# Second MLP's weight blocks: raw words loaded a step ahead, low halves kept in the norm's slots

## The chip, the cores and the metric

The kernel runs on one core of one Trainium2 chip. The metric is the time of one execution on the device in microseconds (us), the median of several runs. A core has five engines that each work through a list of their own, in order: PE (matmuls; its weight loads are shown as PEld), DVE (VectorE), ACT (ScalarE), POOL (GpSimd) and SP, which here only issues DMAs. An engine that waits for a semaphore holds up everything behind it in its list.

## The reference

Attention with two kinds of masks feeds a block with a Fourier mix and an MLP, whose result feeds a token-mixing block with a second MLP:

```
x = attention(q, k, v)                       # 4 batches, 576 tokens, 512 channels
u = x + real(fft(fft(x, tokens), channels))
x = u + relu(norm(u) @ moe_w_ch1) @ moe_w_ch2             # 512 -> 2048 -> 512
u = x + (relu(x^T @ moe2_w_tok1) @ moe2_w_tok2)^T         # 576 -> 256 -> 576
out = u + relu(u @ moe2_w_ch1) @ moe2_w_ch2               # 512 -> 1536 -> 512
```

The weights arrive as float64. The kernel reads them as pairs of 32-bit words.

## The kernel before, in words

The tokens of four batches make 18 tiles of 128 rows. The first MLP works in six chunks c = 0 to 5 of three tiles each, and in 16 slices f of its hidden width. One step (c, f) in `run` is `gemm1` (12 matmuls of 384 columns, L414), an activation that writes `hh`, the high half of the hidden values (ACT, L418), a subtraction that writes `hl`, the low half (DVE, L419), and `gemm2` (9 matmuls of 512 columns, L433). Every product is taken from high and low halves, since PE reads rounded fp32.

Beside the steps of the chunks 2 to 4 the kernel gets the second MLP's weights ready. They are cut into 24 blocks: 12 of w1 (L101's source `in_w1b_dram`) and 12 of w2 (`in_w2b_dram`), one begun every second step, in turns. A block goes through these stages:

- `words` loads four pieces of raw words into a tile `wraw` (SP, L101). ACT takes the absolute value of the high words (L106), four DVE instructions make a float of the pair (L108, L111, L112, L113). The result is `wu`.
- `sums` makes four sums or differences for Strassen's scheme on POOL (L147; w2 has one more, L149) into a tile `wt4`. ACT rounds both to high halves (L153), written back into `wraw`. POOL subtracts to get the low halves `wbl` (L154). Two DMAs store high and low halves to DRAM (`wsd`, L156), from where `load_ops` fetches them for the last stage (L685).

`blocks` is a generator: `begin` runs it to its first pause (loads issued), each `advance` to its next. The pool `wstage` has a ring of three raw buffers (tag "raw") and one of two (tag "wu"). In the kernel before a block takes two of the three raw buffers, one for `wraw` and one for `wbl`:

```
raw = wstage.tile([P, 512, 2], I32, tag="raw", name="wraw", bufs=3)
lo  = wstage.tile([P, 1024], F32R, tag="raw", name="wbl", bufs=3)
```

In the last chunk, c = 5, the six token weights (`load_wt`, `in_wt_dram`) go through `words` and the same rings, and `c_load` begins to split the input of the next stage into `ch` (ACT, L725) and `cl` (DVE or POOL, L726). After the steps come the token products (L785 `tk`, L807 `tu`) and the second MLP (L896, L1037).

The norm of the first MLP takes its output tile `lm` from a ring of three in the pool `lp` (ACT, L485), three times a chunk.

The order of each engine's list is not written out here. The program is recorded in source order, and a scheduler then places instructions by its own model of durations; `behind` adds an order without a wait (L106 and L153 behind the latest `hh`, L108 behind the latest `hl`). So an edit in the source moves instructions on several engines.

Of the kernel before, what the change touches and what calls it, by code (L numbers as in the profile page):

```python
# [10 lines left out]
F32R = mybir.dt.float32r  # L11
# [3 lines left out]
ALU = mybir.AluOpType  # L15
# [3 lines left out]
DM = 512  # L19
P = 128  # L20
# [3 lines left out]
NCH = 6  # L24
# [14 lines left out]
def f32(ap):  # L39
    return ap.bitcast(F32)  # L40
# [3 lines left out]
def attention_fourier_mlp_kernel(ctx: ExitStack, tc: tile.TileContext, a: dict, out: bass.AP):  # L44
    nc = tc.nc

    const = ctx.enter_context(tc.tile_pool(name="const", bufs=1, side="left"))
    wstage = ctx.enter_context(tc.tile_pool(name="wstage", bufs=2, side="left"))
# [17 lines left out]
    wsd = {w: [dram.tile([7, P, 512], F32, name=f"wsd{w}{m}") for m in range(NP2)] for w in "12"}  # L66
# [7 lines left out]
    def behind(ins, prev):  # L74

        if prev is not None:
            tc.add_manual_dep(ins.ins, prev.ins.name, mybir.DependencyInfo(
                mybir.DependencyClass.NoSync, mybir.DependencyReason.SCHED_ONLY), reason="order of the stream")
# [6 lines left out]
    def advance():  # L85
        for x in list(under_way):
            if next(x, None) is None:
                under_way.remove(x)

    def begin(x):  # L90
        next(x)
        under_way.append(x)
# [3 lines left out]
    def words(srcs, eng):  # L96
        raw = wstage.tile([P, 512, 2], I32, tag="raw", name="wraw", bufs=3)
        n = 0
        for src in srcs:
            w = src.shape[1] // 2  # L100
            behind(nc.sync.dma_start(out=raw[:, n:n + w], in_=src.rearrange("p (c t) -> p c t", t=2)), hold[0])  # L101
            n += w
        yield 1
        low, high = raw[:, :n, 0], raw[:, :n, 1]
        u = wstage.tile([P, 512], I32, tag="wu", name="wu", bufs=2)[:, :n]
        behind(nc.scalar.activation(out=f32(u), in_=f32(high), func=AF.Abs, scale=2.0**16), relu.get("hh"))  # L106
        v = nc.vector
        clamp = eng().tensor_scalar(f32(u), f32(u), E_MIN, E_MAX, op0=ALU.max, op1=ALU.min)  # L108
        if eng() is v:
            behind(clamp, relu.get("hl"))  # L110
        v.tensor_scalar(u, u, 4, 1, op0=ALU.logical_shift_left, op1=ALU.logical_shift_right)  # L111
        v.scalar_tensor_tensor(out=u, in0=high, scalar=-2**31, in1=u, op0=ALU.bitwise_and, op1=ALU.bitwise_or)  # L112
        v.scalar_tensor_tensor(out=u, in0=low, scalar=29, in1=u, op0=ALU.logical_shift_right, op1=ALU.bitwise_or)  # L113
        yield f32(u), raw
# [12 lines left out]
    def blocks(w, m, c0):  # L127
        src = a["w" + w + "b"]
        order = ((0, 256), (0, 0), (1, 0), (1, 256)) if w == "2" else ((1, 0), (0, 0), (0, 256), (1, 256))
        x = words([src[m + NP2 * i][:, 2 * (c + c0):2 * (c + c0) + 256] for i, c in order], lambda: nc.vector)  # L130
        yield next(x)
        u, raw = next(x)
        yield 1
        sums(w, m, c0, u, raw)

    def sums(w, m, c0, u, raw):
        q = [u[:, 128 * i:128 * i + 128] for i in range(4)]
        t = wstage.tile([P, 512], F32, tag="wu", name="wt4", bufs=2)
        t1, t2, t3, t4 = (t[:, 128 * i:128 * i + 128] for i in range(4))
        if w == "2":  # L140
            b12, b11, b21, b22 = q
            todo = ((t1, b12, b11, 0), (t2, b22, t1, 0), (t3, b12, b22, 0), (t4, t2, b21, 0))
        else:
            a21, a11, a12, a22 = q
            todo = ((t1, a21, a22, 1), (t2, t1, a11, 0), (t3, a11, a21, 0), (t4, a12, t2, 0))
        for o, x, y, plus in todo:
            nc.gpsimd.tensor_tensor(out=o, in0=x, in1=y, op=ALU.add if plus else ALU.subtract)  # L147
        if w == "2":
            nc.gpsimd.tensor_scalar_mul(q[3], q[3], -1.0)  # L149
        hi = raw.rearrange("p c t -> p (c t)").bitcast(F32R)  # L150
        lo = wstage.tile([P, 1024], F32R, tag="raw", name="wbl", bufs=3)
        for x, s in ((u[:, 128:512], slice(0, 384)), (t, slice(384, 896))):
            behind(nc.scalar.activation(out=hi[:, s], in_=x, func=AF.Copy), relu.get("hh"))  # L153
            nc.gpsimd.tensor_tensor(out=lo[:, s], in0=x, in1=f32(hi[:, s]), op=ALU.subtract)  # L154
        for x, o in ((hi, c0), (lo, 256 + c0)):
            nc.sync.dma_start(out=wsd[w][m][:, :, o:o + 128].rearrange("b p c -> p b c"),  # L156
                              in_=f32(x[:, :896]).rearrange("p (b c) -> p b c", c=128))


    lt = [(0, t) for t in range(6)]  # L160
# [330 lines left out]
    if True:  # L491
# [8 lines left out]
        lp = dst.enter_context(tc.tile_pool(name="ln", bufs=1, side="right"))  # L500
# [28 lines left out]
        f = fp.tile([P, 2, 3, 512], F32R, name="f")  # L529
# [24 lines left out]
        def load_wa():  # L554
            if order:
                x, f = order.pop(0)
                pool, tag = (wa, "wa") if f < 4 else (wx, "wx") if f < 8 else (wb, "wb") if f < 12 else (wc, "wc")
                begin(slot_w(a["w1a" if x == "1" else "w2a"][f], pool, tag, "wA",
                             lambda *t, w=w1 if x == "1" else w2: w.__setitem__(f, t)))
# [20 lines left out]
        for gno, g in enumerate(gl):  # L580
            b, gi = g.b, g.gi
# [54 lines left out]
        def last_fft(x):  # L636
            nonlocal wb, wc
            x4 = four[3]
            prev = relu["hh"], relu["hl"]
            if 2 <= x < 5:  # L640
                x4.prep(x - 2, prev[1], prev[0])
            x4.after = prev
            for mt in {4: (0,), 5: (1, 2), 6: (3, 4)}.get(x, ()):
                x4.s1(mt)
            for i in {7: (0, 1, 2)}.get(x, ()):
                x4.s2(i)
            if x == 8:
                fst.close()
                wb = wbst.enter_context(tc.tile_pool(name="wb", bufs=16, side="left", reuse_waits="tile"))
                wc = wcst.enter_context(tc.tile_pool(name="wc", bufs=16, side="left", reuse_waits="tile"))  # L650
# [8 lines left out]
        def load_wt():  # L659
            n0 = len(wt_names)  # L660
            if n0 < 6:
                nm, i = "12"[n0 // 3], n0 % 3
                wt_names.append(nm)
                src = a["wt" + nm]
                n = min(512, src.shape[1] // 2 - 512 * i)

                def done(hi, lo):
                    wt["h" + nm, i], wt["l" + nm, i] = hi, lo

                begin(slot_w(src[:, 1024 * i:1024 * i + 2 * n], wa, "wa", "wt", done, n))  # L670
# [57 lines left out]
        def c_load(b, ts, late=0):  # L728
            for x, t in enumerate(ts[:4] if b % 2 else ts):
                if late:  # L730
                    begin(c_tile(b, t, late + x // 2))
                else:
                    list(c_tile(b, t, 0))
# [19 lines left out]
        def extra1(c, f):  # L753
            if steps.index((c, f)) <= 8:
                last_fft(steps.index((c, f)))
            advance()
            load_wa()
            if 2 <= c < NCH - 1 and f % 4 == 1:
                m, h = divmod((c - 2) * 4 + f // 4, 2)
                begin(blocks("2", m, 128 * h))  # L760
            if 2 <= c < NCH - 1 and f % 4 == 3:
                m, h = divmod((c - 2) * 4 + f // 4, 2)
                begin(blocks("1", m, 128 * h))
            if c == NCH - 1:
                if f >= 1:
                    load_wt()
                if f == 2:
                    c_load(0, range(3), 3)
                if f == 9:
                    c_load(1, range(5), 3)  # L770

        steps = [(c, f) for h in range(len(PARTS) - 1) for c in range(2) for f in range(PARTS[h], PARTS[h + 1])]
        steps += [(c, f) for c in range(2, NCH) for f in range(NF1)]
        run(m1, steps, prep1, fin1, extra1)


# [452 lines left out]
```

## Time and profile before

| what | value |
|---|---|
| median of 3 runs | 920.49 us (919.70 to 922.67) |
| profiled execution | 919.07 us, of which the span from first to last instruction is 917.3 us |
| PE busy | 889.0 us, 97% of the span |
| DVE, ACT, POOL busy | 561.9, 407.7, 306.7 us |
| granted TensorE clock, mean | 0.994 |

The span is nearly all PE. What is to be had is in PE's few pauses, and these are read by stretch: which stretch has them, and which engine ended each. Times in the rows are counted from the start of the span. The chunks 2 to 4 run from about 300 to 510 us, chunk 5 to about 586 us.

### The profile page before, as it was taken

Reading aid. Unit: us, or ns where it says so; the run is one execution under the profiler, and the core shown is the slowest. Engines: PE = TensorE matmul, PEld = TensorE weight load, DVE = VectorE, ACT = ScalarE, POOL = GpSimd, SP = SyncE. Lnnn points to the kernel's source line nnn. Section 1 sums busy time; section 2 is a strip of 40 time slices with the busy share of each in tenths; the row PEclk is TensorE's granted clock in tenths of the full one; section 3 lists DMA queues with packets and bytes.
Section 4 is the critical chain, followed back from the end, with each engine's and each line's share of the span. In section 5 each row is a group of like instructions: output and inputs, shape, how many; then the busy total and the mean of one; then the engine's idle time right before and its main releaser. Section 6 shows DMA issues by size and latency. Waiting matters only on the chain.

```text
span 917.3 us, 15396 instructions
## 1 busy us (share of the span) xinstructions
PE 889.0 (97%) x5554; PEld 826.3 (90%) x5554; DVE 561.9 (61%) x1049; ACT 407.7 (44%) x1067; POOL 306.7 (33%) x377
## 2 busy tenths in 40 slices
PE   7989998999999999999999999899999999999997
PEld 6979998989998998898988887687999999999997
DVE  4677999797993444534433446846344444898774
ACT  6978884443432233233223224324355545444432
POOL 4431321332330134344344333510113002946660
PEclk9989999999999999999999999999999999999999
DMA  9998764334432444644744766588733287146351
GB/s 264 313 275 256 217 197 134 111 130 144 138 92 70 126 144 139 195 127 131 230 128 133 224 183 183 184 284 293 236 128 147 95 279 235 37 162 226 131 196 46
DMA packets 115987, 159.69 MB, mean 174 GB/s; under 512 B 9643, under 2 KB 69873, under 8 KB 115911
## 3 DMA queue, kind: packets, MB, share of 16 engines
q1 hardware_dynamic: 113111, 153.07, 52.6%
q0 software_dynamic: 2544, 5.42, 2.3%
q8 instruction: 44, 0.72, 0.3%
q14 instruction: 32, 0.26, 0.1%
q10 hardware_dynamic: 256, 0.21, 0.1%
HBM read 103.61 MB, written 55.06 MB: 173 GB/s over the span
## 4 chain that ended last, share of the span: by engine, by line
PE 54%; DVE 11%; DMA 7%; POOL 3%; ACT 3%; issue 3%; SPq 3%; POOLq 0%; DVEq 0%; ACTq 0%
PE oo L1037 14%; PE oo L433 9%; PE h L414 9%; PE z L896 8%; PE y L896 4%; DMA wraw<-in_w1b_dram 4%; POOL wt L147 3%; PE tu L807 3%; DVE wu L112 2%; PE tk L785 2%; PE w L896 2%; DVE wu L113 2%; SPq L101 2%; DVE wu L108 2%; ACT wraw L153 1%
## 5 line engine op out<-in xcount | busy, mean ns | idle before, releaser
L414 PE MATMUL h<-uT,wAh 128*128 128x384 f32 x768 | 203.9, 339 | 0.1
L414 PEld LDWEIGHTS h<-uT,wAh 128*128 128x128 f32 x768 | 139.9, 189 | 4.9 <-DVE uT L404 0.4
L1037 PE MATMUL oo<-wo,ht 128*128 128x256 f32 x972 | 133.7, 281 | 0.0
L414 PE MATMUL h<-uT,wAl 128*128 128x384 f32 x384 | 129.6, 338 | 0.0
L1037 PEld LDWEIGHTS oo<-wo,ht 128*128 128x128 f32 x972 | 126.5, 189 | 0.0
L433 PE MATMUL oo<-wAh,hh 128*128 128x512 f32 x288 | 113.9, 398 | 6.1 <-ACT hh L418 5.4
L433 PE MATMUL oo<-wAl,hh 128*128 128x512 f32 x288 | 113.6, 395 | 0.0
L433 PE MATMUL oo<-wAh,hl 128*128 128x512 f32 x288 | 105.0, 397 | 3.1 <-DVE hl L419 3.1
L419 DVE SCALAR_TENSOR_TENSOR hl<-h,hh 128x384 fp32r<-128x384 f32 x96 | 52.6, 553 | 73.8 <-ACT hh L418 73.4
L108 DVE TENSOR_SCALAR wu<-wu 128x512 f32<-128x512 f32 (+1 forms) x62 | 38.3, 617 | 79.5 <-ACT wu L106 74.5
L124 POOL TENSOR_TENSOR wAl<-wu,wAh 128x512 fp32r<-128x512 f32 x32 | 43.7, 1367 | 105.9 <-ACT wAh L123 69.5
L418 ACT ACTIVATE hh<-h 128x384 fp32r<-128x384 f32 x96 | 45.9, 484 | 66.7 <-PE h L414 65.4
L414 PEld LDWEIGHTS h<-uT,wAl 128*128 128x128 f32 x384 | 72.7, 189 | 2.8
L147 POOL TENSOR_TENSOR wt<-wu 128x128 f32<-128x128 f32 x48 | 21.2, 463 | 160.5 <-DVE wu L113 160.5
L106 ACT ACTIVATE wu<-wraw 128x512 f32<-128x512 f32 (+1 forms) x62 | 41.2, 665 | 67.7 <-DMA wraw<-in_w1b_dram 50.5
L433 PEld LDWEIGHTS oo<-wAh,hh 128*128 128x128 f32 x288 | 54.1, 188 | 18.0 <-ACT hh L418 7.6
L433 PEld LDWEIGHTS oo<-wAh,hl 128*128 128x128 f32 x288 | 53.8, 188 | 17.6 <-DVE hl L419 5.4
L896 PE MATMUL z<-ut,wo 128*128 128x384 f32 x324 | 64.4, 338 | 0.4 <-ACT snap L903 0.4
L231 ACT ACTIVATE sm<-sc,st 96x128 f32<-96x128 f32 (+2 forms) x176 | 61.7, 373 | 0.6
L433 PEld LDWEIGHTS oo<-wAl,hh 128*128 128x128 f32 x288 | 54.1, 188 | 8.6
L896 PEld LDWEIGHTS z<-ut,wo 128*128 128x128 f32 x324 | 56.4, 188 | 0.8 <-ACT snap L903 0.8
L112 DVE SCALAR_TENSOR_TENSOR wu<-wraw,wu 128x512 int32<-128x512 int32 (+1 forms) x62 | 52.7, 850 | 1.1
(204 smaller groups left out, 1823.9 us busy)
## 6 DMA issues: line engine op xcount, KB each, us to landing
wo<-wsd SPq DMA_DIRECT2D x84, 256.0 KB
wsd<-wraw SPq DMA_DIRECT2D x24, 448.0 KB
wsd<-wbl SPq DMA_DIRECT2D x24, 448.0 KB
hd<-hs SPq DMA_DIRECT2D x12, 768.0 KB
hw<-hd SPq DMA_DIRECT2D x36, 256.0 KB
wraw<-in_w1a_dram SPq DMA_DIRECT2D x16, 512.0 KB
wraw<-in_w2a_dram SPq DMA_DIRECT2D x16, 512.0 KB
u<-u2d SPq DMA_DIRECT2D x30, 256.0 KB
```

Source lines behind the costliest of these rows:

```text
L106: behind(nc.scalar.activation(out=f32(u), in_=f32(high), func=AF.Abs, scale=2.0**16), relu.get("hh"))
L108: clamp = eng().tensor_scalar(f32(u), f32(u), E_MIN, E_MAX, op0=ALU.max, op1=ALU.min)
L112: v.scalar_tensor_tensor(out=u, in0=high, scalar=-2**31, in1=u, op0=ALU.bitwise_and, op1=ALU.bitwise_or)
L124: nc.gpsimd.tensor_tensor(out=lo[:, :n], in0=u, in1=f32(hi[:, :n]), op=ALU.subtract)
L147: nc.gpsimd.tensor_tensor(out=o, in0=x, in1=y, op=ALU.add if plus else ALU.subtract)
L231: self.exp = nc.scalar.activation(out=smv[:, j, :], in_=sc[:, j, :], func=AF.Exp, scale=SCALE, bias=st[:, 1, j:j + 1], accum_out=st[:, 2, ...
L414: nc.tensor.matmul(out=h[:, :384], lhsT=l[:, ws], rhs=r[:, kd, :], start=x == 0, stop=x == 11)
L418: relu["hh"] = nc.scalar.activation(out=hh, in_=h[:, :384], func=AF.Relu)
L419: relu["hl"] = nc.vector.scalar_tensor_tensor(out=hl, in0=h[:, :384], scalar=0.0, in1=f32(hh), op0=ALU.max, op1=ALU.subtract)
L433: nc.tensor.matmul(out=self.o[c][i], lhsT=l[:, s], rhs=r, start=first and x == 0, stop=last and x == 2)
L896: Unit.last = nc.tensor.matmul(out=bank[:, :384], lhsT=w[:, c + kd * P:c + kd * P + P], rhs=r[:, kd], start=first and x == 0, stop=x == 5, ...
L1037: nc.tensor.matmul(out=acc[G][bank][:, 256 * half:256 * half + 256], lhsT=lh[:, i], rhs=w[:, c:c + 256], start=m == 0 and x == 0 and half ...
```

## The change

Three edits. The load of a block's raw words is begun ahead of `advance()` in `extra1`, hence ahead of the sums of the block before it, and a pause is added behind the load so that the other stages stay in the steps in which they were. The low halves are taken from the norm's ring "lm" (two tiles a block, of 384 and 512 columns) and no longer from the ring "raw". The low halves are stored by two DMAs, so a block now issues three stores where it issued two; bytes are the same.

```diff
@@ blocks
         yield next(x)
+        for _ in range(1):
+            yield 1
         u, raw = next(x)
@@ sums
-        lo = wstage.tile([P, 1024], F32R, tag="raw", name="wbl", bufs=3)
+        los = []
         for x, s in ((u[:, 128:512], slice(0, 384)), (t, slice(384, 896))):
             behind(nc.scalar.activation(out=hi[:, s], in_=x, func=AF.Copy), relu.get("hh"))
-            nc.gpsimd.tensor_tensor(out=lo[:, s], in0=x, in1=f32(hi[:, s]), op=ALU.subtract)
-        for x, o in ((hi, c0), (lo, 256 + c0)):
-            nc.sync.dma_start(out=wsd[w][m][:, :, o:o + 128].rearrange("b p c -> p b c"),
-                              in_=f32(x[:, :896]).rearrange("p (b c) -> p b c", c=128))
+            lo = lp.tile([P, DM], F32R, tag="lm", name="wbl", bufs=3)[:, :s.stop - s.start]
+            nc.gpsimd.tensor_tensor(out=lo, in0=x, in1=f32(hi[:, s]), op=ALU.subtract)
+            los.append(lo)
+        for x, r, o in ((hi[:, :896], slice(0, 7), c0), (los[0], slice(0, 3), 256 + c0), (los[1], slice(3, 7), 256 + c0)):
+            nc.sync.dma_start(out=wsd[w][m][r, :, o:o + 128].rearrange("b p c -> p b c"),
+                              in_=f32(x).rearrange("p (b c) -> p b c", c=128))
@@ extra1
+            if 2 <= c < NCH - 1 and f % 2:
+                m, h = divmod((c - 2) * 4 + f // 4, 2)
+                begin(blocks("2" if f % 4 == 1 else "1", m, 128 * h))
             advance()
             load_wa()
-            if 2 <= c < NCH - 1 and f % 4 == 1:
-                m, h = divmod((c - 2) * 4 + f // 4, 2)
-                begin(blocks("2", m, 128 * h))
-            if 2 <= c < NCH - 1 and f % 4 == 3:
-                m, h = divmod((c - 2) * 4 + f // 4, 2)
-                begin(blocks("1", m, 128 * h))
```

SP's list in the middle of the blocks, before. A number behind a name tells one buffer's use from the next; `wsd1..` is w1, `wsd2..` is w2.

```order
L156 DMA wsd22_89<-wraw_4398 128x7x128
L101 DMA wraw_4474<-in_w1b_dram 128x256 x3
L156 DMA wsd22_89<-wbl_4467 128x7x128
L101 DMA wraw_4474<-in_w1b_dram 128x256
L101 DMA wraw_4549<-in_w2b_dram 128x256 x4
L156 DMA wsd12_83<-wraw_4474 128x7x128
L156 DMA wsd12_83<-wbl_4542 128x7x128
```

The same place after:

```order
L160 DMA wsd22_89<-wraw_4400 128x7x128
L160 DMA wsd22_89<-wbl_4489 128x3x128
L160 DMA wsd22_89<-wbl_4492 128x4x128
L101 DMA wraw_4632<-in_w1b_dram 128x256 x4
L160 DMA wsd12_83<-wbl_4566 128x3x128
L160 DMA wsd12_83<-wraw_4477 128x7x128
L160 DMA wsd12_83<-wbl_4569 128x4x128
L101 DMA wraw_4729<-in_w2b_dram 128x256 x4
```

Before, the w1 block `wraw_4474` is loaded just behind the store of the block ahead of it, and is itself the next to be stored. After, the load behind the store of `wraw_4400` is that of `wraw_4632`, and two other blocks (`wraw_4477`, `wraw_4555`) are worked on before it is needed.

ACT's list around two blocks, before (`hh` once a step):

```order
L106 ACTIVATE wu_4351<-wraw_4314 128x512
L418 ACTIVATE hh_4457<-h_4444 128x384
L418 ACTIVATE hh_4501<-h_4488 128x384
L153 ACTIVATE wraw_4314<-wu_4351 128x384
L153 ACTIVATE wraw_4314<-wt4_4386 128x512
L418 ACTIVATE hh_4533<-h_4520 128x384
L106 ACTIVATE wu_4429<-wraw_4398 128x512
L418 ACTIVATE hh_4576<-h_4563 128x384
L153 ACTIVATE wraw_4398<-wt4_4461 128x512
L153 ACTIVATE wraw_4398<-wu_4429 128x384
L418 ACTIVATE hh_4608<-h_4595 128x384
L418 ACTIVATE hh_4652<-h_4639 128x384
```

And after:

```order
L106 ACTIVATE wu_4966<-wraw_4921 128x512
L422 ACTIVATE hh_4994<-h_4981 128x384
L155 ACTIVATE wraw_4921<-wt4_5003 128x512
L155 ACTIVATE wraw_4921<-wu_4966 128x384
L422 ACTIVATE hh_5046<-h_5033 128x384
L106 ACTIVATE wu_5050<-wraw_4998 128x512
L422 ACTIVATE hh_5081<-h_5068 128x384
L155 ACTIVATE wraw_4998<-wu_5050 128x384
L422 ACTIVATE hh_5126<-h_5113 128x384
L155 ACTIVATE wraw_4998<-wt4_5090 128x512
```

Two blocks had five `hh` with them before and have four after: the blocks now go at the pace of the steps, one block every two steps, and the last of them stand at the start of chunk 5 instead of in the middle of it.

## Rows read from the trace of the kernel before

**Rows 1.** Stretches: length, then busy us of PE, PEld, DVE, ACT, POOL; clock; DMA share; GB/s

```profile
300.00:560.00 260.00, 255.37 (x1290) 228.33 (x1290) 110.35 (x203) 78.87 (x157) 103.27 (x157) 1.00 0.53 159
560.00:590.00 30.00, 26.06 (x120) 21.42 (x120) 26.84 (x36) 13.43 (x27) 14.87 (x10) 1.00 0.61 189
```

**Rows 2.** What PE waited for, 300 to 560: us, times, longest

```profile
PE oo L433 <- ACT hh L418: 4.6, 4, 1.7
```

**Rows 3.** What PE waited for, 560 to 590: us, times, longest

```profile
PE oo L433 <- DVE hl L419: 3.1, 3, 1.9
PE oo L433 <- ACT hh L418: 0.8, 1, 0.8
```

**Rows 4.** Timeline of ACT: start, us, instruction, [idle before, by whom ended]

```profile
427.84 0.66 ACT L106 ACTIVATE wu<-wraw 128x512 f32<-128x512 f32 x1 [6.02 <-DMA wraw<-in_w1b_dram]
...
431.38 0.85 ACT L418 ACTIVATE hh<-h 128x384 fp32r<-128x384 f32 x2
...
434.27 0.65 ACT L106 ACTIVATE wu<-wraw 128x512 f32<-128x512 f32 x1
...
440.30 0.63 ACT L153 ACTIVATE wraw<-wt 128x512 fp32r<-128x512 f32 x1 [5.00 <-POOL wt L147]
```

**Rows 5.** Timeline of PE at the same place

```profile
429.97 0.34 PE L414 MATMUL h<-uT,wAl 128*128 128x384 f32 x1
431.91 0.50 PE L433 MATMUL oo<-wAh,hh 128*128 128x512 f32 x1 [1.60 <-ACT hh L418]
432.25 0.39 PE L433 MATMUL oo<-wAl,hh 128*128 128x512 f32 x1
```

**Rows 6.** Chain that ended last: start, us, piece

```profile
299.99 2.08 PE h L414 x12
302.08 2.10 PE oo L433 x9
...
338.21 3.91 DMA wraw<-in_w1b_dram
```

**Rows 7.** What ACT waited for, 300 to 600: us, times, longest

```profile
ACT wraw L153 <- POOL wt L147: 63.9, 23, 5.0
ACT wu L106 <- DMA wraw<-in_w1b_dram: 50.5, 12, 6.5
```

**Rows 8.** L106 in 300 to 562: duration min/median/max in ns, first and last start

```profile
L106 ACT ACTIVATE wu<-wraw x25: 642/660/674, 306.7 to 559.5; 128x512 f32<-128x512 f32 x25
```

**Rows 9.** Timeline of POOL at the place of rows 4

```profile
434.44 1.30 POOL L154 TENSOR_TENSOR wbl<-wt,wraw 128x512 fp32r<-128x512 f32 x1 [0.74 <-ACT wraw L153]
...
442.27 1.02 POOL L154 TENSOR_TENSOR wbl<-wu,wraw 128x384 fp32r<-128x384 f32 x1
```

**Rows 10.** Timeline of DVE at the same place

```profile
428.53 0.43 DVE L108 TENSOR_SCALAR wu<-wu 128x512 f32<-128x512 f32 x1 [6.63 <-ACT wu L106]
...
430.18 0.69 DVE L113 SCALAR_TENSOR_TENSOR wu<-wraw,wu 128x512 int32<-128x512 int32 x1
...
435.01 1.01 DVE L108 TENSOR_SCALAR wu<-wu 128x512 f32<-128x512 f32 x1 [2.10 <-issue]
```

**Rows 11.** Timeline of ACT, a slow w2 block

```profile
369.33 0.65 ACT L106 ACTIVATE wu<-wraw 128x512 f32<-128x512 f32 x1
...
376.90 0.63 ACT L153 ACTIVATE wraw<-wt 128x512 fp32r<-128x512 f32 x1 [3.99 <-POOL wt L147]
```

**Rows 12.** Timeline of all engines in chunk 5

```profile
570.52 0.63 ACT L725 ACTIVATE ch<-cr 128x512 fp32r<-128x512 f32 x1 [1.75 <-DMA cr<-x2d]
...
572.66 1.75 POOL L124 TENSOR_TENSOR wtl<-wu,wth 128x512 fp32r<-128x512 f32 x1
...
573.17 1.78 DVE L113 SCALAR_TENSOR_TENSOR wu<-wraw,wu 128x512 int32<-128x512 int32 x1
```

**Rows 13.** SP: issue of a store at the place of rows 4

```profile
434.39 0.38 SPq L156 DMA_DIRECT2D wsd<-wraw  x1
```

**Rows 14.** Chain that ended last, whole span: a store

```profile
560.96 3.27 DMA wsd<-wbl
```

## The prediction

> **What bounds the kernel now.** I read the stretches first, then PE's waits, then the lists of the engine that ends them. PE is busy for 255.37 of the 260 us from 300 to 560 and for 26.06 of the 30 us behind it, at a granted clock of 1.00, the upper of its two levels, throughout [rows 1]. So PE is the bound and no other engine's busy share matters by itself: what the change can give is PE's idle time here, nothing else. PE's waits say who ends it: `hh` from ACT four times, 4.6 us [rows 2], then in chunk 5 `hl` from DVE, 3.1 us, and `hh` once more, 0.8 us [rows 3]. Together 8.5 us, which agrees with the two stretches (4.63 + 3.94 = 8.57).
>
> Why is `hh` late? ACT's timeline at one of the four: L106 sat 6.02 us until the raw words of a w1 block had landed, and the `hh` that PE wanted stood behind it and ran only at 431.38 [rows 4]; PE went on at 431.91 [rows 5]. The chain shows the same on another pair of blocks: the load of w1 words alone is 3.91 us of it [rows 6]. All 12 w1 blocks cost ACT such a wait, 50.5 us in total, up to 6.5 [rows 7]. The wait exists because the raw ring has three buffers and a block takes two: the w1 load can't start until the block ahead has stored, and the block wants the words at once.
>
> In chunk 5 it is another thing: the blocks are late as a whole. Their first L106 is at 306.7, and L106 still runs at 559.5 [rows 8], in the middle of chunk 5, so the token weights' words and the split of the next input fall together on DVE, busy for 26.84 of 30 us [rows 1]. There `hl` comes late.
>
> **The change part by part.** *The raw ring.* With the low halves gone from it, three raw buffers serve three blocks. SP's list after the change loads a block's words when the block three ahead of it has stored, so two other blocks, of two steps each, lie between load and use. A step is 2.08 + 2.10 = 4.18 us of PE [rows 6], so the words have some 16 us to land in, and a load took 3.91. ACT's wait at L106 goes, and with it the 4.6 us of rows 2.
>
> *What the idle view leaves out.* The matmul before the stall starts at 429.97 and the next at 431.91, 1.94 apart, where 12 such matmuls take 2.08, 0.17 each [rows 5, 6]: 1.77 lost against 1.60 shown. The next start is 0.34 later where nine take 2.10, 0.23 each: 0.11 more. So each stall costs 0.28 beyond its idle time, 2.2 us for eight. Ceiling of the gain: 8.5 + 2.2 = 10.7 us.
>
> *Pace of the blocks.* Two blocks had five `hh` among them in ACT's list and now have four. What is late next is therefore the chain of the blocks itself, which has to fit into four steps, 16.7 us, plus a norm tile's transposes. From rows 4 a w1 block takes 434.27 - 427.84 = 6.43 us from its L106 to the next block's. A w2 block takes 440.30 - 434.27 = 6.03 to its first L153, 0.63 for that, about 0.5 for the second (384 of 512 columns), about 0.1 to POOL and 1.02 for the low half of `wu` [rows 4, 9], which now stands ahead of that of `wt4` in POOL's list and frees the buffer that the next L106 writes: 8.3. With one `hh` ahead (half of the 0.85 of the two at 431.38), a pair takes 15.2 us. It fits, by 1.5. A slow w2 block needed 376.90 - 369.33 = 7.57 instead of 6.03 [rows 11], and L108 took 1.01 instead of 0.43 beside a POOL subtraction [rows 9, 10]: a pair with both mishaps takes 15.2 + 1.54 + 0.58 = 17.3, 0.6 too long. This is covered: in both programs' lists a step's `hh` is used one whole step (21 matmuls, 4.2 us) behind the matmul that completes `h`. A 5.00 us wait of ACT for POOL's sums at 440.30 cost PE nothing for that reason [rows 4].
>
> *Chunk 5.* Blocks that keep the steps' pace end with the first steps of chunk 5, some 40 us earlier. The token weights' words then run beside an otherwise light DVE, and the 3.1 us of `hl` go. The 0.8 us of `hh` I keep: there ACT sat 1.75 us for a `cr` load just ahead of `hh` [rows 12], and the new list has the same `ch` in front of the same `hh`.
>
> *The three stores.* 24 more issues at 0.38 us [rows 13] are 9 us of SP. A block costs SP three stores and four loads, about 2.9 us out of 8.4; bytes and subtractions are as before. I take nothing for it.
>
> *The norm's ring.* A low half now waits until the store out of its buffer has landed, one block (8.4 us) earlier. Issue and landing are 0.38 + 3.27 [rows 13, 14], and if SP first waits for a raw buffer and issues four loads, 5.2. About 3 us of margin; POOL would wait, and ACT behind it. The cost lies between nothing and the whole 4.6 us of rows 2 with their restarts. I take 1.4 us for this ring and for pairs that run long, nearer to nothing because the nearest row (the 5.00 us wait) cost nothing.
>
> **Sum.** 10.7 less the `hh` of chunk 5 (0.8 + 0.28 = 1.1) less 1.4 is 8.2 us. The profiled execution took 919.07, so 910.9. The median of the runs shown is 1.42 above that execution; I forecast 912.3 us for the median.
>
> **Rivals.** *Half of it.* ACT's waits move from the load to the norm's ring or to POOL, and the four stalls of chunks 2 to 4 come back in their old size, 4.6 + 4 x 0.28 = 5.7 us. Chunk 5 alone is won: 3.1 + 3 x 0.28 = 3.9, so 920.49 - 3.9 = 916.6. For it: ACT's waits for POOL's sums are the longer ones already, 63.9 us against 50.5 [rows 7], and they remain. Against: a stall needs more than 4.2 us of delay, and the sums wait is short when the block starts in time.
>
> *No change.* PE's waits keep their sum and merely change their names, in chunk 5 too, because the denser blocks keep ACT and DVE as busy. 920.5. Against: DVE has 110 us of work in 260 and POOL 103 [rows 1]; a quarter more fits.
>
> *Slower: the blocks throttle PE.* In chunk 5 a word instruction, L113, took 1.78 us instead of 0.69 [rows 10] while a POOL subtraction of 1.75 us ran from 572.66 [rows 12]. If every block meets this, with L108 at 1.01 as well, a pair grows by 2 x (0.58 + 1.09) less the 0.58 that the w2 block of rows 4 holds already, that is 2.76, and a slow w2 block in one pair of four adds 0.4: 18.4 us. Four `hh` per pair stand in ACT's list, so PE then runs at 18.4 instead of 16.7: 12 x 1.7 = 20.4, less the one step in hand, 16.2. Against the 10.7 won that is 5.5 slower, 926.0 us. It decides where a pair passes 17.9 (12 x 1.2 = 14.9 = 10.7 + 4.2). Against it: L106 starts only when the low half of `wu` is done, so just that of `wt4`, 1.30 us [rows 9], is left to collide, and L106 (0.66) covers half of it.
>
> The Trainium skill ("SBUF — State Buffer", section "Who interferes with whom") says that VectorE instructions with two SBUF inputs, or in a two-port mode, and GpSimd instructions lock each other out of a shared port for a whole instruction. Rows 9, 10 and 12 agree with it (1.01 and 1.78 us beside POOL). By that rule any denser mix of the two is dearer than the rows of quiet blocks say, which is this rival.
>
> **Chances and range.** My forecast 0.67, its own range 910 to 915.5 (ceiling 10.7 below the median is 909.8). Half 0.17, no change 0.07, slower 0.09. A measurement of this kernel can tell about 0.3%, 2.8 us, from no change. The forecast and some 0.6 of the half lie beyond that: faster 0.77. The rest of the half and no change: 0.14. Slower 0.09. For 8 in 10 the range goes from 909.2, just below the ceiling, to 919, which takes in the half and leaves out no change and slower.
>
> **What would show it.** Right: the waits of L106 for w1 loads fall from 50.5 us to nearly nothing; PE waits under 1 us for `hh` from 300 to 560; the last block's L106 comes some 30 us earlier, near 525, and the token words follow it at once; PE's wait for `hl` in chunk 5 is gone; and everything behind chunk 5 starts some 8 us earlier at unchanged pace. Wrong: a POOL subtraction L157 or the norm's `lm` waiting for a DMA `wsd<-wbl`; pairs of L106 more than 17.9 us apart; or a new PE wait between 590 and 650, where the token products would meet inputs that are not ready.

## The result, and the profile after

| | device us, median | runs | ratio to before |
|---|---|---|---|
| before | 921.34 | 4, 919.7 to 922.67 | |
| changed | 908.62 | 4, 904.85 to 911.78 | 0.9861 [0.9816, 0.9906] |

The change makes the kernel faster by 12.7 us. The forecast was 912.3 with a range from 909.2: the direction and the mechanism hold, but the time lies 0.6 us below the range.

The stretches of [rows 1] in the profile after, and the one behind them. The columns are the same:

```profile
300.00:560.00 260.00, 260.00 (x1324) 235.29 (x1323) 132.89 (x236) 93.27 (x181) 113.45 (x165) 1.00 0.60 177
560.00:590.00 30.00, 30.00 (x135) 24.82 (x134) 9.09 (x14) 7.84 (x14) 8.16 (x7) 1.00 0.45 150
590.00:650.00 60.00, 58.99 (x309) 51.42 (x308) 28.22 (x41) 20.39 (x35) 2.66 (x2) 1.00 0.76 257
```

The first busy column is PE: it has no idle time left up to 590. DVE, 26.84 us busy from 560 to 590 before, is down to 9.09. What PE waits for from 300 to 650 is this alone, and both waits lie near 622 (us, times, longest):

```profile
PE tu L808 <- DVE hl L799: 0.6, 1, 0.6
PE z L897 <- ACT snap L904: 0.4, 1, 0.4
```

All eight waits of [rows 2, 3] are gone. What ACT waits for from 300 to 590 answers to [rows 7]:

```profile
ACT hh L422 <- PE h L418: 125.2, 56, 7.3
ACT wraw L155 <- POOL wt L149: 18.6, 13, 2.5
ACT ch L729 <- DMA cr<-x2d: 12.4, 6, 4.7
...
ACT wu L106 <- POOL wbl L157: 0.5, 1, 0.5
```

The 50.5 us of L106 for the words of w1 blocks are not in the list any more, the wait for the sums falls from 63.9 us (in the slightly longer window of [rows 7]) to 18.6, and the idle time stands where it costs nothing: ACT is early and waits for PE's `h`. The timeline of ACT over two blocks shows it (compare [rows 4], where L106 had 6.02 us of idle time before it and PE's `hh` stood behind it):

```profile
374.35 0.65 ACT L106 ACTIVATE wu<-wraw 128x512 f32<-128x512 f32 x1
377.63 0.49 ACT L422 ACTIVATE hh<-h 128x384 fp32r<-128x384 f32 x1 [2.63 <-PE h L418]
380.61 0.63 ACT L155 ACTIVATE wraw<-wt 128x512 fp32r<-128x512 f32 x1 [2.49 <-POOL wt L149]
381.15 0.51 ACT L155 ACTIVATE wraw<-wu 128x384 fp32r<-128x384 f32 x1
381.82 0.49 ACT L422 ACTIVATE hh<-h 128x384 fp32r<-128x384 f32 x1 [0.16 <-PE h L418]
382.80 0.66 ACT L106 ACTIVATE wu<-wraw 128x512 f32<-128x512 f32 x1 [0.49 <-POOL wbl L157]
385.99 0.49 ACT L422 ACTIVATE hh<-h 128x384 fp32r<-128x384 f32 x1 [2.53 <-PE h L418]
```

**Where the time came from.** Two marks can be read in every profile: chunk 2's first `hh` on ACT, and the first `z` matmul on PE, which stands behind chunk 5 and the token products. Before:

```profile
300.03 0.49 ACT L418 ACTIVATE hh<-h 128x384 fp32r<-128x384 f32 x1 [1.15 <-PE h L414]
634.46 0.60 PE L896 MATMUL z<-ub,wo 128*128 128x384 f32 x2
```

After:

```profile
296.93 0.49 ACT L422 ACTIVATE hh<-h 128x384 fp32r<-128x384 f32 x1 [1.59 <-PE h L418]
619.80 0.42 PE L897 MATMUL z<-ub,wo 128*128 128x384 f32 x1
```

From mark to mark: 334.4 us before, 322.9 after. A mark between the chunks has to be on PE, since a late `hh` on ACT would shift it. Chunk 5's first `h` matmul serves: from chunk 2's first to it PE does as many matmuls of each kind in both programs. Before:

```profile
505.42 0.34 PE L414 MATMUL h<-uT,wAh 128*128 128x384 f32 x1
```

After:

```profile
497.09 0.34 PE L418 MATMUL h<-uT,wAh 128*128 128x384 f32 x1
```

With it and chunk 5's last `oo` (starts from the timelines, in us):

| stretch | before | after | won |
|---|---|---|---|
| start to chunk 2's first `hh` | 300.03 | 296.93 | 3.1 |
| from there to chunk 5's first `h` matmul | 205.39 | 200.16 | 5.2 |
| chunk 5, to its last `oo` | 80.28 | 73.86 | 6.4 |
| from there to the first `z` | 48.77 | 48.85 | -0.1 |
| from the first `z` to the span's end | 282.8 | 283.3 | -0.4 |

The sum is 14.2, as the two profiled executions differ (919.07 and 904.85). The first row is not the change's: up to there nothing that the diff touches runs, and over twelve profiles of this study, whatever the kernel, chunk 2 began between 296.9 and 305.8. Part of that goes with the granted clock. In every one of the twelve it was at 0.50 for some stretches within the first 160 us, for 3.4 us in all in the changed kernel's profile and for 10.2 in that of the kernel before (the seventh figure is the clock; before, then after):

```profile
60.00:66.80 6.80, 5.44 (x28) 5.33 (x29) 6.35 (x19) 5.27 (x24) 3.25 (x2) 0.50 0.93 246
142.00:145.40 3.40, 3.40 (x11) 3.40 (x12) 2.81 (x8) 0.10 (x1) 0.00 (x0) 0.50 0.25 75
```

```profile
137.40:140.80 3.40, 3.27 (x11) 2.92 (x12) 2.93 (x7) 2.16 (x5) 1.28 (x1) 0.50 0.28 90
```

Half of the 6.8 us between them is 3.4, an estimate that would cover the 3.1; profiles with the same time at 0.50 still differ by up to 3.5 us in where chunk 2 begins, so the clock is not all of it. The other four rows are the change: 11.1 us.

### The profile page after: what moved, and what is told of

Same layout as the page of the kernel before. It is cut to its first block, busy times and chain, and to the rows that moved or that the text cites. A ratio compares the mean times of both kernels' runs of the same rounds, so it can differ in the third digit from the quotient of the medians.

```text
span 903.1 us, 15462 instructions
## 1 busy us (share of the span) xinstructions
PE 884.7 (98%) x5554; PEld 824.5 (91%) x5554; DVE 561.4 (62%) x1049; ACT 409.2 (45%) x1067; POOL 305.5 (34%) x377
## 4 chain that ended last, share of the span: by engine, by line
PE 80%; DVE 4%; DMA 0%; issue 0%; POOL 0%; ACT 0%; DVEq 0%; POOLq 0%
PE oo L437 21%; PE h L418 21%; PE oo L1038 15%; PE z L897 8%; PE y L897 4%; PE tu L808 3%; PE tk L786 3%; PE w L897 2%; PE ut L846 1%; PE ut L404 1%; DVE wu L112 1%; PE fa L365 1%; PE fb L365 1%; PE g L339 0%; DVE wu L111 0%; DVE wu L113 0%
## 5 line engine op out<-in xcount | busy, mean ns | idle before, releaser
L418 PE MATMUL h<-uT,wAh 128*128 128x384 f32 x768 | 207.0, 338 | 0.0
L904 ACT ACTIVATE snap<-z 128x384 f32<-128x384 f32 x54 | 26.1, 488 | 51.3 <-PE z L897 51.0
L216 PE MATMUL sc<-k,qz 128*96 128x128 f32 (+2 forms) x352 | 48.2, 276 | 0.3 <-DMA k<-in_kt_dram 0.2
```

The source lines that it names most:

```text
L216: last = nc.tensor.matmul(out=sc[:q, j * k:(j + 1) * k], lhsT=qz[self.g][:, e, hp, qs], rhs=k_t[self.b, self.g][:, hp, ks], start=False, s ...
L418: nc.tensor.matmul(out=h[:, :384], lhsT=l[:, ws], rhs=r[:, kd, :], start=x == 0, stop=x == 11)
```

## The experiments

"c2 to z" below is the stretch between the two marks. It leaves out the start, which scatters by more than the effects looked for.

| kernel | c2 to z, us | PE waits from 300 to 590, us | device us |
|---|---|---|---|
| before, profiled | 334.4 | 8.5 | 919.07 |
| before_again | 335.9 | 9.6 | 922.47 |
| after, profiled | 322.9 | 0 | 904.85 |
| after_again | 322.9 | 0 | 909.25 median, 0.988 [0.9847, 0.9913] |
| ring_only | 322.9 | 0 | 912.02 median, 0.9899 [0.9855, 0.9942] |
| early_only | 323.4 | 0.4 | 908.25 median, 0.9856 [0.9814, 0.9898] |
| blocks_8_steps_late | 324.4 | 0.9 | 910.85 |
| blocks_14_steps_late | 332.8 | 2.3 | 917.20 |
| low_half_twice | 322.9 | 0 | 906.42 |
| hold_act_10 | 322.7 | 0 | 909.56 |
| hold_act_17 | 337.9 | 11.1 | 925.06 |
| hold_act_24 | 376.2 | 35.3 | 966.92 |

Medians are of several runs beside the kernel before, the other times of one.

**Which half of the change does it?** *ring_only* is the changed kernel with the load begun where it was:

```diff
         def extra1(c, f):
+            advance()
+            load_wa()
             if 2 <= c < NCH - 1 and f % 2:
                 begin(blocks(...))
-            advance()
-            load_wa()
@@ blocks
-        for _ in range(1):
-            yield 1
```

> Low halves in the norm's ring and stored by two DMAs, but a block's load is begun behind the sums of the block before it, as in the kernel before, and the pause behind it is taken out. Measure: PE's waits from chunk 2 to chunk 5, and the stretch from chunk 2's first hh to the first z matmul (before 334.5 us, after 322.9). Theory A (PE stalled because ACT's L106 waited for raw words, and the shared raw ring is what made them late): the ring alone frees the loads; no PE wait in chunks 2 to 5, the stretch 322 to 325 us, the time within 3 us of the changed kernel. Theory B (what counts is where in the program the load is begun): the w1 loads stay late, PE waits of 4 us or more remain, the stretch 329 to 335 us.

*early_only* is the kernel before with the load begun a step ahead and the pause, and the low halves still in the raw ring:

```diff
         def extra1(c, f):
+            if 2 <= c < NCH - 1 and f % 2:
+                begin(blocks(...))
             advance()
             load_wa()
-            if 2 <= c < NCH - 1 and f % 4 == 1: ...
-            if 2 <= c < NCH - 1 and f % 4 == 3: ...
@@ blocks
+        for _ in range(1):
+            yield 1
```

> The load begun ahead of the sums, with the pause behind it, but the low halves in the raw ring and one store for them, as in the kernel before. Theory A: the load now stands one block ahead (some 8 us) instead of none, a load takes 3 to 4 us; L106's waits for raw words fall from 50 us to under 15, PE waits in chunks 2 to 5 fall from 8.5 to under 3 us, the stretch 323 to 327 us. Theory B' (the ring is all): a block still takes two of three buffers, pairs of blocks stay about 21 us apart, the stretch 331 to 336 us.

Measured: no PE wait in ring_only and one of 0.4 us in early_only, stretches of 322.9 and 323.4. Each half alone gives the whole gain: early_only is 0.56 us longer up to the first `z` and 0.44 shorter behind it (282.8 us, as in the kernel before, where ring_only has the 283.3 of the changed kernel). L106 waits for no words of w1 blocks in either. The intervals of the two ratios overlap, and their profiled executions differ in the start (305.8 and 300.5 to chunk 2), which neither half touches. The load has only to leave the place where ACT needs it at once, and either way does that.

**How much of it is scatter?** Both kernels were profiled a second time, unchanged.

> The changed kernel again. Of the 14.2 us between the two profiled spans, 3.1 lay ahead of chunk 2, where both programs have the same instructions in the same order. Theory C (that part is the difference of two runs): chunk 2's first hh comes anywhere from 294 to 304 us in this profile, while the stretch from there to the first z is 322.9 within 0.6. Theory D (the change makes the first 300 us shorter): the first hh of chunk 2 comes at 296.9 within 1 us, and in the kernel before at 300 within 1. The time 905 to 912 us in both.

> The kernel before again, one profile. Theory C: chunk 2's first hh between 294 and 304 us, the stretch from there to the first z 334.5 within 1, PE waits in chunks 2 to 5 again 8 to 9 us. Theory D: first hh at 300 within 1 us.

The changed kernel's stretch came out the same to 0.01 us, 322.87 twice, while its start differed by 3.0. The kernel before did not repeat so: 335.9 instead of 334.4, with PE's waits from 300 to 600

```profile
PE oo L433 <- ACT hh L418: 5.9, 6, 1.5
PE oo L433 <- DVE hl L419: 3.7, 5, 1.8
```

9.6 us against the 8.5 of [rows 2, 3]. Both miss what was expected, 334.5 within 1 and 8 to 9. Here the stretch in which PE never waits repeated; the one with stalls did not. That the landing of DMAs makes the difference fits [rows 7], but was not tested.

**Was it lateness that made the waits of chunk 5?** *blocks_8_steps_late* and *blocks_14_steps_late* are the changed kernel with every block begun so many steps later (8 shown):

```diff
-            if 2 <= c < NCH - 1 and f % 2:
-                m, h = divmod((c - 2) * 4 + f // 4, 2)
+            t = 16 * (c - 2) + f - 8
+            if 0 <= t < 48 and f % 2:
+                m, h = divmod(t // 4, 2)
```

> The changed kernel with all 24 blocks begun 8 steps later, so that the last third of the w1 and w2 blocks runs into chunk 5 up to its eighth step, as in the kernel before, at the new pace. Measure: PE waits from chunk 2 to the first z, and that stretch (322.9 us in the changed kernel, 334.5 and 335.9 in the one before). Theory A (chunk 5's waits for hl come because the blocks, the token weights' words and the next input's split fall together): PE waits of 3 to 5 us, all in chunk 5, the stretch 326 to 329 us. Theory B (they came from the shared raw ring, which held up the token words): no PE wait over 0.5 us, the stretch 322.5 to 324 us.

> The changed kernel with every block begun 14 steps later (58.5 us) instead of 8, so that the token weights' words end where those of the kernel before did: their last L106 some 287 us behind chunk 2's first hh, against 285.7 in the kernel before and 262.4 with 8 steps. Theory A (lateness itself makes the waits of chunk 5; 8 steps were merely not late enough): PE waits of 2.5 us or more in chunk 5 for hl or hh, and a stretch from chunk 2's first hh to the first z matmul of 326.5 us or more. Theory B (the waits of chunk 5 need the shared raw ring, in which token words stand behind the blocks' low halves): PE waits of 1.2 us or less in chunk 5, stretch at most 325 us, as with 8 steps (0.9 and 324.4).

With 8 steps, PE's waits from 300 to 590 are

```profile
PE oo L437 <- DVE hl L423: 0.9, 2, 0.7
```

and with 14, from 500 to 680,

```profile
PE oo L437 <- DVE hl L423: 2.3, 3, 1.3
PE tu L809 <- DVE u L816: 1.1, 1, 1.1
PE tu L809 <- ACT hh L799: 0.8, 1, 0.8
PE ut L847 <- DMA u<-u2d: 0.6, 1, 0.6
```

From chunk 5's first `h` matmul to its last `oo` this is 75.28 and 76.95 us, 1.4 and 3.1 over the changed kernel, where the kernel before stood 6.4 over. With 14 steps the last L106 is 296.2 us behind chunk 2's first `hh`, later than the 285.7 of the kernel before, and yet lateness cost 3.1 of the 6.4. The shared raw ring without lateness cost less still: early_only stands 0.65 over in chunk 5. So the rest seems to need both. The two together (early_only, late) were not tried, and the denser order of these kernels differs from that of the kernel before, so this part is argued by exclusion, not shown. Of the two theories for 14 steps neither came true in full: 2.3 us of waits lie between their bounds. What neither had: up to the first `z` 14 steps cost 6.8 us more behind the last `oo` (55.6 instead of 48.85). Of this 5.3 come back behind the first `z` (278.0 instead of 283.3), since 18 `tu` matmuls that stood behind it now stand ahead of it; to the span's end 14 steps cost 4.6 us. The stretch of 332.8 would have looked like theory A; the split shows that most of it lies elsewhere.

**Is the pairs' margin as thin as the sum said?** *low_half_twice* computes the low half of `wt4` twice on POOL in every block:

```diff
-            nc.gpsimd.tensor_tensor(out=lo, in0=x, in1=f32(hi[:, s]), op=ALU.subtract)
+            for _ in range(1 + len(los)):
+                nc.gpsimd.tensor_tensor(out=lo, in0=x, in1=f32(hi[:, s]), op=ALU.subtract)
```

> The changed kernel with POOL's 512-column low half subtracted twice in each block, 1.30 us of POOL more per block, 2.6 per pair. Theory A (the chain of a pair as added up in the prediction, 15.2 us, has only 1.5 us to spare against PE's four steps): a pair takes 17.8, 12 x 1.1 less the 4.2 in hand is 9 us, PE waits of about that, the stretch 330 to 334 us. Theory B (that sum is too long: this subtraction runs beside L106 and the word instructions of the next block): pairs of L106 stay 16.7 to 17.3 us apart, no PE wait, the stretch 322.5 to 324 us.

Groups of DVE and POOL from 300 to 505 in the changed kernel (busy us, mean ns | idle before):

```profile
L108 DVE TENSOR_SCALAR wu<-wu 128x512 f32<-128x512 f32 x24 | 13.3, 553 | 3.1 <-ACT wu L106 2.9
L111 DVE TENSOR_SCALAR wu<-wu 128x512 int32<-128x512 int32 x24 | 10.2, 426 | 0.7
L157 POOL TENSOR_TENSOR wbl<-wt,wraw 128x512 fp32r<-128x512 f32 x23 | 29.8, 1294 | 8.0 <-ACT wraw L155 8.0
```

and in low_half_twice:

```profile
L108 DVE TENSOR_SCALAR wu<-wu 128x512 f32<-128x512 f32 x23 | 19.2, 835 | 4.9 <-ACT wu L106 4.7
L111 DVE TENSOR_SCALAR wu<-wu 128x512 int32<-128x512 int32 x23 | 20.5, 891 | 0.7
L158 POOL TENSOR_TENSOR wbl<-wt,wraw 128x512 fp32r<-128x512 f32 x45 | 59.3, 1318 | 8.1 <-ACT wraw L155 6.4
```

The second subtraction, 1.3 us, runs beside the next block's word instructions: L111 takes 891 ns in the mean instead of 426 and L108 835 instead of 553. One by one, L111 took about 1.4 us at 11 of 23 blocks, and it or L108 took over 0.6 us at 19, against 6 of 24 in the changed kernel. So collisions like that of [rows 10] were brought about at most blocks, and PE waited for nothing. The pairs did not get longer: from the first block's L106 to the last's it is 199.3 us, against 198.4 in the changed kernel. L113, which took 1.78 us in [rows 12], was not slowed (at most 694 ns).

**How late may `hh` come?** *hold_act_10*, *hold_act_17* and *hold_act_24* put that many activations of 256 columns on a scratch tile behind L106 of each w1 block, 12 times, with the next `hh` behind the last:

```diff
-        behind(nc.scalar.activation(out=f32(u), in_=f32(high), func=AF.Abs, scale=2.0**16), relu.get("hh"))
+        x = nc.scalar.activation(out=f32(u), in_=f32(high), func=AF.Abs, scale=2.0**16)
+        behind(x, relu.get("hh"))
+        if slow:
+            for i in range(slow.pop()):
+                y = nc.scalar.activation(out=junk, in_=junk if i else f32(high[:, :256]), func=AF.Abs)
+                behind(y, x)
+                x = y
+            last_slow.append(x)
...
+        if w == "1":
+            slow.append(10)
```

(the list `slow` gets 10, 17 or 24 at a w1 block; the lines that put the next `hh` behind `last_slow` are left out here).

> The changed kernel with ten 256-column activations on a scratch tile between L106 of each w1 block and the next hh, about 0.37 us each, so ACT is held 3.7 us there, 12 times; hh found ACT idle for about 2.5 us there before, so it comes about 1.2 us late. Theory A (hh is used one step, 4.2 us, behind the matmul that completes h): no PE wait, the stretch 322.5 to 324 us. Theory B (PE stops as soon as hh is late): 12 x 1.2 us and more, the stretch 336 us or more.

> The changed kernel with 17 extra activations of 256 columns (0.45 us from start to start, 7.6 us) behind L106 of each w1 block, 12 times, and the next hh behind the last of them. Without the hold ACT stood about 2.5 us idle ahead of that hh until PE had finished h, so hh comes some 5.1 to 6 us later than it could. Theory A (one whole step in hand, 4.2 us): PE waits 0.9 to 1.8 us at most w1 blocks, 8 to 20 us in chunks 2 to 5, stretch 333 to 347 us. Theory B (24 activations stalled PE because the blocks as a whole ran late, not by the hold of a single hh; with 17 a pair of blocks still fits into four steps): waits under 3 us, stretch at most 326 us. Beside both: if the granted clock of 0.5 in the run with 24 followed the length of the stalls, 4.7 us at the longest, it does not show here, with stalls under 2 us.

> The same with 24 such activations, ACT held about 8.9 us, hh about 6.4 us late. Theory A: beyond the 4.2 us in hand PE waits some 2.2 us, 12 times, with the 0.28 of a restart each about 30 us, the stretch 348 to 358 us; PE waits name hh. Theory B: 12 x 6.4, the stretch 395 us or more.

An extra activation took 0.45 us from start to start, not the 0.37 first expected. Ten (4.5 us) cost nothing. 17 (7.6 us) cost PE, from 300 to 590,

```profile
PE oo L450 <- ACT hh L433: 11.1, 9, 2.1
```

and 24 (10.8 us)

```profile
PE oo L450 <- ACT hh L433: 35.3, 12, 4.7
```

So theory A, a whole step in hand, holds in sign in all three, and in size for 17: 7.6 less the 2.5 us that ACT waited for `h` anyway less 4.2 leaves 0.9 a time, and 11.1 / 12 is 0.93 in the mean (single waits run from none to 2.1). For 24 the same sum gives 4.1 a time and the waits were 2.9, which was not followed up. The stretch grew by 53.4 us instead of the expected 25 to 35; of these 35.3 are waits and 12 x 0.28 = 3.4 restarts. The other 14.7 fit the lower clock (last section). With 17, 11.1 + 9 x 0.28 = 13.6 and 1.7 for one stretch of 3.4 us at half clock make 15.3; measured 15.1.

## Why the prediction was right or wrong

The mechanism held, but two terms that the sum held back were mis-sized: 1.1 us for the `hh` of chunk 5 and 1.4 us for the norm's ring and long pairs. Both measured nothing. The gain behind the start is 11.1 us where the sum had 8.2, and the lower end of the range, cut to the ceiling of one execution, left no room for scatter.

*PE is the bound and its idle time is the gain: right.* The stalls went and nothing took their place; PE is busy for 260.00 of 260.

*The raw ring and the restarts: the cause right, the split misread.* The prediction put all four stalls of [rows 2] into chunks 2 to 4, 5.7 us with their restarts. But those rows reach to 560, and the fourth stall lies in chunk 5, which begins at 505.42:

```profile
552.76 0.50 PE L433 MATMUL oo<-wAh,hh 128*128 128x512 f32 x1 [0.77 <-ACT hh L418]
```

So chunks 2 to 4 hold three, 3.8 us, and 4.6 with 3 x 0.28; measured 5.2. Chunk 5 holds five, 4.7 us, and 6.1 with 5 x 0.28; measured 6.4. In both more came back than the restart of 0.28, read at a single stall, gives: 11.6 won for 8.5 of waits is about 0.4 a stall, an estimate that puts the whole rest on the restarts. L106's wait for w1 words went from 50.5 us to none. That three free buffers do it was only half of the reason: early_only, where the ring is still shared, does it too.

*The `hh` of chunk 5, 1.1 us kept: wrong.* The wait for `cr` ahead of it was taken for the cause. In the changed kernel the same pattern is there, longer, and costs nothing:

```profile
562.53 0.63 ACT L729 ACTIVATE ch<-cr 128x512 fp32r<-128x512 f32 x1 [2.06 <-DMA cr<-x2d]
564.15 0.49 ACT L422 ACTIVATE hh<-h 128x384 fp32r<-128x384 f32 x1 [0.99 <-PE h L418]
```

Behind a wait of 2.06 us `hh` still stands 0.99 us early. In the kernel before, the `hh` of [rows 12] was late because ACT had, since the last one, also waited for token words and run two of their L106:

```profile
566.82 0.67 ACT L106 ACTIVATE wu<-wraw 128x512 f32<-128x512 f32 x1 [1.78 <-DMA wraw<-in_wt_dram]
...
568.10 0.68 ACT L106 ACTIVATE wu<-wraw 128x512 f32<-128x512 f32 x1
570.52 0.63 ACT L725 ACTIVATE ch<-cr 128x512 fp32r<-128x512 f32 x1 [1.75 <-DMA cr<-x2d]
571.06 0.47 ACT L418 ACTIVATE hh<-h 128x384 fp32r<-128x384 f32 x1
```

By the rule that the prediction itself used, a delay of 1.75 us cannot eat a step of 4.2; the delays add up, and the change takes the others away. Chunk 5 gave 6.4 us, where its five stalls without this `hh` come to 5.0.

*The norm's ring and long pairs, 1.4 us: wrong, nothing.* No wait for a store out of the norm's ring shows on POOL. What its low halves wait for, from 300 to 590, is

```profile
POOL wbl L157 <- ACT wraw L155: 26.5, 25, 2.6
```

and the long pairs are carried by the step in hand. The term was made by choosing a value between nothing and 4.6 although the nearest row said nothing.

*The pair of blocks, 15.2 us: its margin was larger than that.* A further 1.3 us of POOL in each of its two blocks would have made it 17.8, above the 16.7 of four steps; low_half_twice showed no PE wait. The sum counted in a row what can run side by side, the low half beside L106 and DVE's words. Single pairs did come 18.1 and up to 19.7 us apart, past the 17.9 that was named as a sign of being wrong, and cost nothing: the three chunks take 204.5 us on ACT and hold twelve, 17.04 each.

*Slower, by collisions of DVE and POOL: rightly unlikely.* By the Trainium skill ("SBUF — State Buffer", section "Who interferes with whom") a GpSimd instruction and a VectorE instruction in a two-port mode lock each other out of a shared port. low_half_twice agrees in so far as L111 got longer (426 to 891 ns in the mean). No `hh` came late enough by that to stop PE. The full price of the rival was not tried, since its larger term, L113 at 1.78 us, came up nowhere from 300 to 505 (at most 695 ns in the changed kernel, 694 in low_half_twice).

*Blocks end earlier and chunk 5 is relieved: right in direction, too small in size, and as a cause shown for half of it.* The prediction took the L106 at 559.5 of [rows 8] for a block's; it is a token weight's, the last block's is at 551.7, and the last of all at 585.7. Blocks and token words together now end at 531.1:

```profile
L106 ACT ACTIVATE wu<-wraw x30: 435/661/678, 303.5 to 531.1; 128x512 f32<-128x512 f32 x29, 128x256 f32<-128x256 f32 x1
```

The last block's L106 is at 501.9, 50 us earlier than before, where the prediction had some 30 and a place near 525. Lateness brought back 3.1 of chunk 5's 6.4 us; what makes the rest stays open.

*The range.* With both kept terms at nothing the sum would have been 920.49 - 10.7 = 909.8, and with the measured 11.1 it is 909.4, inside the range. The other 0.8 down to 908.62 is no effect of the change that could be shown: the two profiles of the changed kernel differ by 3.0 us, all of it in the first 300 us, its times run from 904.85 to 913.04, and the stalls of the kernel before vary from 8.5 to 9.6. In the four runs behind the 908.62 the time falls as the mean granted clock rises: 911.78 us at 0.989, 910.20 at 0.994, 907.03 at 0.997, 904.85 at 0.998. Where in that spread a median of four falls is luck. Putting the lower end just below one execution's ceiling left no room for either. In the later runs beside one another the medians were 919.74 before (11 runs) and 909.25 after (6 runs), 10.5 apart.

## What to carry to other kernels

A stall is the sum of all that its engine did since the last time it was early, not the wait that stands just ahead of it; ask how much slack the steady state has (here one step of 4.2 us, measured with a hold that costs nothing at 4.5 us and 0.9 a time at 7.6) before keeping part of a stall. When one kernel has stalls and the other's are gone, the first may vary where the second repeats, so measure the change between two marks around it, and make the range wider than one profile's idle time. A load that is wanted at once can be freed by issuing it earlier or by giving it a buffer; here one of the two was enough.

## What the runs showed of the hardware

The granted clock fell to its lower level at or behind stalls, which the expectations had not counted. In hold_act_17 PE stood 2.12 us, and half a microsecond later the clock fell for 3.4 us:

```profile
364.80 0.34 PE L429 MATMUL h<-uT,wAl 128*128 128x384 f32 x1
367.25 0.50 PE L450 MATMUL oo<-wAh,hh 128*128 128x512 f32 x1 [2.12 <-ACT hh L433]
```

The stretches around it (the seventh figure is the clock):

```profile
357.80:367.80 10.00, 7.88 (x45) 7.35 (x44) 3.93 (x8) 9.04 (x23) 2.91 (x6) 1.00 0.47 134
367.80:371.20 3.40, 3.40 (x10) 2.69 (x9) 2.59 (x5) 1.66 (x4) 2.14 (x2) 0.50 0.64 178
371.20:381.20 10.00, 10.00 (x52) 9.02 (x51) 5.67 (x10) 6.14 (x14) 5.16 (x9) 1.00 0.66 199
```

At 0.50, 1.2 GHz, PE does 10 matmuls in 3.40 us; at 1.00, 52 in 10. In hold_act_24 nine of the twelve stalls went with such a stretch, two of them of 6.8 us, 37.4 us together. Six began up to 1.3 us behind the stall, three while PE still stood, as here in one of 4.7 us that ended at 356.46:

```profile
346.00:354.50 8.50, 5.73 (x35) 5.38 (x33) 1.56 (x3) 7.30 (x18) 1.75 (x4) 1.00 0.27 82
354.50:361.30 6.80, 4.84 (x12) 3.97 (x13) 3.97 (x11) 4.96 (x12) 2.25 (x2) 0.50 0.46 126
```

PE was busy for 33.1 of the 37.4, and half of that is 16.5, an estimate of the cost; 14.7 was left over in the sum. The length of a stall alone did not decide it: in hold_act_24 one of 1.79 us was followed by a fall and one of 3.07 was not, and in hold_act_17 a second stall of 2.11 was not. The expectation of hold_act_17 that stalls of about 2 us might leave the clock alone did not hold. The kernel before, with stalls up to 1.94 us, kept 1.00 through chunks 2 to 5.
